# PV moved behind the MoE products of its step and one step further from its scores, with at most one MoE unit a step and a shorter distance in the last batch

## Chip, cores and metric

One NeuronCore of a Trainium2 chip runs the whole program. The metric is the device time of one execution in microseconds, median of several runs. Before the change it was 582.16 us (three runs, 581.99 to 584.43). An execution counts as slow here when it is over 1.5% above the fastest of the same kernel.

## The reference

Eight batches of attention with a threshold, then a two-layer MoE block over all tokens.

```python
scores = (1 / sqrt(64)) * q @ k.T                     # 8 batches, 8 heads, 576 x 576, head dim 64
thresh = max(scores, axis=-1) - tau                   # tau = 0.02
scores = where(scores >= thresh, scores, -1e9)
attn   = exp(scores - max) / (sum + 1e-9)
x      = (attn @ v)  as  4608 tokens x 512
h      = x @ w_in                                     # 512 -> 2048
out    = maximum(0.01 * h, h) @ w_out                 # 2048 -> 512, float32
```

## The kernel before

The engines are PE (matrix products), DVE (vector), ACT (activations), POOL (GpSimd) and SP (which issues DMAs). The program is written as one long software pipeline of 144 steps. A step computes the scores of 128 query rows for two heads; the 64 rows left over of a batch, the ragged block, go through two steps of four heads each. What happens to one step's scores, and when:

- step s: PE makes the scores (`sc`, one PSUM buffer a head). DVE scales them to `sf` with the row maximum (`mx`, then `bb`). ACT and POOL each subtract the maximum from one head's half and write the 16-bit tile `P`.
- step s+1: DVE clamps `P` as int16 (in place, `P<-P`), ACT takes the exponential into `w` with the row sums.
- step s+2: DVE takes the reciprocal of the sums (`rc`), writes it beside the weights (`w<-rc`), and the SP queue issues a DMA transpose `wt<-w`. A unit of two steps, 128 x 2560 half-precision values, is transposed at once in batches 2 to 6; batches 0 and 1, and the second half of the last, use units of one step, except for the ragged blocks.
- step s+LAG: PE multiplies the transposed weights with V (`pv`), DVE evacuates the product with the normalisation (`xT`).
- Later: the MoE. An `h` unit is 8 or 16 products into `hp`, a relu on ACT, and a leaky sum `gT` on DVE. An `o` unit is 4 products into `op`; every fourth ends in a copy `osb` and a store. Units wait in two queues and are fed one of each a step.

Each engine executes in the order in which this loop records its instructions.

```python
LAG = 5; BONUS = 0.25; NW = 4; NWT = 4; WOUT = 1; OSB_ACT = False
...
for ui in range(len(units)):
    last = units[ui][3] + size[ui] - 1
    pv_at.setdefault(EARLY.get(ui, last + LAG), []).append(ui)       # EARLY is empty
...
for s in range(NS + LAG + 1):
    credit = min(credit + 1.0 + BONUS * (len(hq) + len(oq) > 8), 2.0)
    hu, ou, fins = [], [], []
    while credit >= 1.0:            # one h and one o unit, with a backlog now and then two
        ...
    if live:
        sc = [...]                  # PE: scores
        scores(s, sc)
    ...                             # DVE: two maxima, bb; ACT and POOL: P
    leak()                          # DVE: gT of the h unit of the step before
    evacs = [pv(ui) for ui in pv_at.get(s, [])]                      # PE: PV
    for i in range(max(len(ou), len(hu))):
        if i > 0:
            leak()
        o = ou[i]() if i < len(ou) else None                         # PE: op
        h = hu[i]() if i < len(hu) else None                         # PE: hp
        if i == 0:
            for f in evacs:
                f()                                                  # DVE: xT
            evacs = []
        for f in (h, o):
            ...                                                      # ACT: relu; DVE: osb
    for f in evacs:
        f()
    ...                             # DVE: rc, w of the unit done a step ago; SP: transpose wt
    ...                             # DVE: P<-P of the step before; ACT: exp
    ...                             # loads and preparation of the next batch's q, k, v
# after the last step: the remaining o and h units, in turn
```

Of the kernel before, what the change touches and what calls it, by code (L numbers as in the profile page):

```python
# [16 lines left out]
def kernel(  # L17
# [26 lines left out]
    DM = moe_w_in.shape[0]  # L44
    DF = moe_w_in.shape[1]
    C = 1.0 / (64.0 * 64.0 * 8.0)
    LAG = 5
    NARROW = 2
    NJ = DF // 128
    NEG = -1025.0  # L50
# [1 line left out]
    NWT = 4  # L52
    NW = 4
    NP_ = 3
    BONUS = 0.25
    OSB_ACT = False
    WOUT = 1
    PT = 0
    SPOOL = 4
# [159 lines left out]
    def leak():  # L219
        for G, u, hp in leaky:  # L220
            nc.vector.scalar_tensor_tensor(  # L221
                out=G.g[u], in0=hp, scalar=0.01, in1=G.g[u], op0=AX.mult, op1=AX.add)

            nj = 512 // G.n
            nv = (u + 1) * nj // 4
            if (u + 1) * nj % 4 == 0:
                oq.append((lambda G=G, v=nv - 1: o_unit(G, v), G.n))
            if u == NJ // nj - 1:
                for v in range(NJ // 4, G.n // 32):
                    oq.append((lambda G=G, v=v: o_unit(G, v), G.n))  # L230
        leaky.clear()
# [3 lines left out]
    def osb_act():  # L235
        return OSB_ACT

# [72 lines left out]
    def group_of(b, blk):  # L310

        key = (b, blk) if blk != (4,) else ("t", b // 2)
        if key not in groups:
            groups[key] = Group([rows_of(b - b % 2 if c == 4 else b, c) for c in blk], b)
        return groups[key], (64 * (b % 2) if blk == (4,) else 0), blk != (4,) or b % 2 == 1
# [32 lines left out]
    def pv(ui):  # L348
        b, blk, p, _ = units[ui]
        wt = uwt[ui]  # L350
        vt = vts[b]
        nw = size[ui]
        if npv[0] % 2 == 0:
            pvt[0] = ps.tile([128, 2, 256], FP32, tag="pv", bufs=1, name="pv")
        pvp = pvt[0][:, npv[0] % 2, :]
        npv[0] += 1
        if p is not None:
            parts = [(p, wt[:, 0:nw, :, :], pvp[:, 0 : 128 * nw].rearrange("f (i r) -> f i r", i=nw))]
        else:
            parts = [(2 * i + u, wt[:, i : i + 1, :, ds(64 * u, 64)], pvp[:, ds(64 * (2 * i + u), 64)].rearrange("f (i r) -> f i r", i=1))  # L360
                     for i in range(2) for u in range(2)]
        for pp, w_, o_ in parts:
            for j in range(5):
                for h in range(2):
                    nc.tensor.matmul(  # L365
                        out=o_[ds(64 * h, 64)], lhsT=vt[:, pp, h, j, :], rhs=w_[:, :, 4 * h + j, :],
                        start=(j == 0), stop=(j == 4), skip_group_check=True, tile_position=(0, 64 * h))
        G, col, done = group_of(b, blk)

        def evac():  # L370


            if p is not None:
                for c in range(nw):
                    nc.vector.tensor_tensor(  # L375
                        out=G.x[:, p, ds(128 * c, 128)].rearrange("f (p i) -> f i p", i=2),
                        in0=pvp[:, ds(128 * c, 128)].rearrange("f (i p) -> f i p", i=2),
                        in1=wt[:, c, 9, :].rearrange("f (i p) -> f i p", i=2), op=AX.mult)
            else:
                x_ = G.x.rearrange("f g (p i) -> f g i p", i=2)[:, :, col // 64, :]  # L380
                nc.vector.tensor_tensor(
                    out=x_.rearrange("f (a u) p -> f a u p", u=2),
                    in0=pvp.rearrange("f (a u p) -> f a u p", a=2, u=2),
                    in1=wt[:, 0:2, 9, :].rearrange("f a (u p) -> f a u p", u=2), op=AX.mult)
            if done and (p is None or p == NP - 1):
                for u in range(NJ * G.n // 512):
                    hq.append((h_unit(G, u), G.n))

        return evac
# [11 lines left out]
    def at(s, f, t=tick):  # L401
        t.setdefault(max(0, s), []).append(f)
# [55 lines left out]
    for b in range(1, B):  # L458
        s0 = 18 * (b - 1)
        for hb in range(2):  # L460
# [7 lines left out]
            i = 0  # L468
            for nm in "kq":
                for h in range(2):  # L470
                    at(t0 + i + PT, lambda nm=nm, h=h, b=b, hb=hb: after_anchor(x64(nm, b, hb, h)), ptick)

                    def f(nm=nm, h=h, b=b, hb=hb):
                        for part in PARTS[nm]:
                            after_anchor(lo(nm, b, hb, h, part))
# [6 lines left out]

    for g in range(8):
        at(WOUT + g // 2, lambda g=g: load_w_out(g))
    EARLY = {}
    pv_at = {}
    for ui in range(len(units)):
        last = units[ui][3] + size[ui] - 1
        pv_at.setdefault(EARLY.get(ui, last + LAG), []).append(ui)

    credit = 0.0
    stores = []
# [1 line left out]
    done = None  # L494
    for s in range(NS + LAG + 1):
        live = s < NS
        for f in stores:
            f()
        stores = []

        credit = min(credit + 1.0 + BONUS * (len(hq) + len(oq) > 8), 2.0)
        hu, ou, fins = [], [], []
        while credit >= 1.0:
            f = next_o()
            if f:
                ou.append(f)
            f = next_h()
            if f:
                hu.append(f)
            credit -= 1.0  # L510

        if live:
            sc = [ps.tile([128, 1024], FP32, tag=f"sc{h}", bufs=1, name=f"sc{h}") for h in range(2)]
            scores(s, sc)
        last, prev = prev, None
        if live:
            P_ = sb.tile([128, 2, 576], FP16, tag="P", bufs=NP_, name="P")
            mx = sb.tile([128, 2], FP32, tag="mx", bufs=4, name="mx")
            sa, sB = smax(0, sc, mx), smax(1, sc, mx)
            bb = sb.tile([128, 2], FP32, tag="bb", bufs=4, name="bb")  # L520
            nc.vector.tensor_scalar(out=bb, in0=mx, scalar1=-1.0, scalar2=tau_f, op0=AX.mult, op1=AX.add)  # L521
            nc.scalar.activation(out=P_[:, 1, :], in_=sB, func=AF.Identity, bias=bb[:, 1:2], scale=1.0)  # L522
            (nc.vector if s < SPOOL else nc.gpsimd).tensor_scalar(  # L523
                out=P_[:, 0, :], in0=sa, scalar1=1.0, scalar2=bb[:, 0:1], op0=AX.mult, op1=AX.add)
            prev = (P_,) + unit_of[s]
        leak()
        evacs = [pv(ui) for ui in pv_at.get(s, [])]
        for i in range(max(len(ou), len(hu))):
            if i > 0:
                leak()  # L530
            o = ou[i]() if i < len(ou) else None
            h = hu[i]() if i < len(hu) else None
            if i == 0:
                for f in evacs:
                    f()
                evacs = []
            for f in (h, o):
                if f:
                    g_ = f()
                    if callable(g_):  # L540
                        stores.append(g_)
        for f in evacs:
            f()
        now, done = done, None
        if now is not None:
            nw = size[now]
            rc = sb.tile([128, 2, 2], FP32, tag="rc", bufs=3, name="rc")
            nc.vector.reciprocal(out=rc[:, 0:nw, :], in_=usm[now][:, 0:nw, :])  # L548
            W_ = uW[now][:, 0:nw, :]
            nc.vector.tensor_scalar(  # L550
                out=W_[:, :, 1152:1280].rearrange("p i (h r) -> p i h r", h=2),
                in0=rc[:, 0:nw, :].unsqueeze(3).to_broadcast([128, nw, 2, 64]), scalar1=1.0, scalar2=None, op0=AX.mult)
            uwt[now] = sb.tile([128, 2, 10, 128], FP16, tag="wt", bufs=NWT, name="wt")
            nc.sync.dma_start(
                out=uwt[now][:, 0:nw].rearrange("p i j r -> p (i j) r"), in_=W_.rearrange("p i c -> p (i c)"),
                transpose=True)
        if last is not None:
            P_, ui, i = last
            pi = P_.bitcast(mybir.dt.int16)
            anchor[0] = nc.vector.tensor_scalar(out=pi, in0=pi, scalar1=NEG, scalar2=None, op0=AX.max)  # L560
            if i == 0:
                uW[ui] = sb.tile([128, 2, 1280], FP16, tag="w", bufs=NW, name="w")
                usm[ui] = sb.tile([128, 2, 2], FP32, tag="sm", bufs=NW, name="sm")
            for h in range(2):
                nc.scalar.activation(  # L565
                    out=uW[ui][:, i, ds(576 * h, 576)], in_=P_[:, h, :], func=AF.Exp, bias=exp_bias, scale=1.0,
                    accum_out=usm[ui][:, i, h : h + 1])
            if i == size[ui] - 1:
                done = ui
        for t in ptick.get(s, []):  # L570
            t()
        for t in tick.get(s, []):
            t()
# [5 lines left out]
    while hq or oq or leaky:  # L579
        for nx in (next_o, next_h):  # L580
            leak()
            f = nx()
            if f:
                f = f()
# [39 lines left out]
```

## Time and profile before

The first fence is one row of the table of groups (line, engine, operation, tiles, shapes, count, then busy us and mean ns of one, then idle time before it). The second is the window view, with the run cut at the start of step 18 and of step 143; after each engine's busy time the columns are granted clock (PE's, 1.00 is full speed), DMA share and GB/s.

```profile
L560 DVE TENSOR_SCALAR P<-P 128x1152 int16<-128x1152 int16 x144 | 68.1, 473 | 0.0
```

```profile
0.00:83.60 83.60, 57.54 (x626) 37.53 (x626) 64.14 (x187) 57.85 (x117) 45.24 (x68) 0.81 1.05 195
83.60:536.90 453.30, 398.14 (x4368) 249.94 (x4369) 399.06 (x1164) 357.22 (x782) 205.85 (x269) 0.96 1.00 183
536.90:577.40 40.50, 31.99 (x336) 21.21 (x334) 17.42 (x36) 12.32 (x25) 0.75 (x1) 1.00 0.25 63
```

I call these three stretches the head, the loop (125 steps) and the tail. In the loop DVE is busy 399.06 us of 453.30 (third number with a count), so it idles 54.2 us; PE is busy 398.14. Neither engine is full.

### The profile page before, as it was taken

To read this page: it belongs to the slowest core of one execution; us is meant where nothing else is said; L and a number is where in the kernel's file an instruction comes from. 1 tells how busy PE (TensorE), PEld (TensorE's weight loads), DVE (VectorE), ACT (ScalarE), POOL (GpSimd) and SP (SyncE) were. 2 spreads that over 40 slices of the span, in tenths; PEclk is the share of its full clock that TensorE was granted. 3 is DMA by queue.
4 is the path that set the end of the run, shared out by engine and by line. 5 is a ranking of instruction groups with operands and counts; after the bars stand their busy time and mean duration, and the time that the engine had idled before them with its cause. 6 is when DMAs were issued, how large, how long until landed. Compare 5 with 4: busy or idle time off the path is not lost.

```text
span 577.4 us, 14379 instructions
## 1 busy us (share of the span) xinstructions
PE 487.7 (84%) x5328; PEld 308.7 (53%) x5328; DVE 480.6 (83%) x1385; ACT 427.4 (74%) x922; POOL 251.8 (44%) x338
## 2 busy tenths in 40 slices
PE   5549879989898779888989898976899798999896
PEld 4326546556565445555555555634566465655573
DVE  5848987999899877998879988987789799898742
ACT  5748876888789667887879877886779688787621
POOL 5335851477236741476226842376225762222100
PEclk9756988999999788998999999989899899999999
DMA  8999799999999998899997999799997999657601
GB/s 213 190 223 232 135 175 173 202 245 193 165 221 201 183 181 133 181 230 187 177 223 177 201 188 184 153 231 171 168 190 145 238 197 169 111 121 135 141 19 54
DMA packets 280133, 101.85 MB, mean 176 GB/s; under 512 B 254976, under 2 KB 267264, under 8 KB 280064
## 3 DMA queue, kind: packets, MB, share of 16 engines
q1 hardware_dynamic: 267008, 92.03, 82.9%
q0 software_dynamic: 13056, 8.92, 11.7%
q8 instruction: 41, 0.67, 0.5%
q14 instruction: 28, 0.23, 0.1%
HBM read 36.70 MB, written 9.44 MB: 80 GB/s over the span
## 4 chain that ended last, share of the span: by engine, by line
DVE 38%; DMA 27%; PE 23%; ACT 7%; issue 3%; SPq 0%; ACTq 0%
DMA wt<-w 26%; DVE sf L394 16%; PE op L239 8%; DVE gT L221 7%; PE hp L239 7%; DVE P L560 4%; ACT w L565 4%; PE sc L334 4%; DVE w L550 4%; PE pv L365 4%; DVE osb L275 3%; DVE xT L375 2%; DVE bb L521 1%; DMA qm<-in_q_dram 1%; DVE rc L548 1%
## 5 line engine op out<-in xcount | busy, mean ns | idle before, releaser
L394 DVE TENSOR_SCALAR_CACHE_REDUCE sf<-sc 128x576 f32<-128x576 f32 x288 | 205.7, 750 | 37.8 <-PE sc L334 30.0
L565 ACT ACTIVATE w<-P 128x576 f16<-128x576 f16 x288 | 193.9, 675 | 37.1 <-DVE P L560 33.5
L523 POOL TENSOR_SCALAR P<-sf,bb 128x576 f16<-128x576 f32 x140 | 106.5, 760 | 217.7 <-DVE bb L521 213.9
L239 PE MATMUL op<-wout,gT 128*128 128x512 f16 x576 | 153.4, 391 | 3.8 <-DVE osb L275 3.5
L239 PE MATMUL hp<-xT,win 128*128 128x128 f16 (+1 forms) x1600 | 155.6, 247 | 0.1
L334 PE MATMUL sc<-kst,qst 64*128 64x320 f16 (+1 forms) x1536 | 136.2, 298 | 17.1 <-DVE sf L394 13.8
L239 PEld LDWEIGHTS <-win 128*128 128x128 f16 x1600 | 125.7, 100 | 42.1 <-issue 5.6
L522 ACT ACTIVATE P<-sf,bb 128x576 f16<-128x576 f32 x144 | 111.3, 773 | 44.5 <-DVE bb L521 41.4
L253 ACT ACTIVATE gT<-hp 128x512 f16<-128x512 f32 x144 | 83.8, 583 | 55.0 <-PE hp L239 55.0
L221 DVE SCALAR_TENSOR_TENSOR gT<-hp,gT 128x512 f16<-128x512 f32 x144 | 98.5, 684 | 18.8 <-ACT gT L253 18.6
L334 PEld LDWEIGHTS <-qst 64*128 64x128 f16 x1536 | 73.7, 97 | 69.3 <-issue 44.2
L365 PE MATMUL pv<-wt,v 128*64 128x256 f16 (+2 forms) x1160 | 61.9, 246 | 57.5 <-DMA wt<-w 53.2
L365 PEld LDWEIGHTS <-v 128*64 128x64 f16 x1160 | 45.3, 114 | 77.0 <-issue 56.8
L239 PEld LDWEIGHTS <-gT 128*128 128x128 f16 x576 | 47.4, 99 | 62.9 <-issue 24.7
L560 DVE TENSOR_SCALAR P<-P 128x1152 int16<-128x1152 int16 x144 | 68.1, 473 | 0.0
L565 ACT ACTIVATION_READ_ACCUMULATOR w<-P 128x1 f32 x288 | 54.0, 188 | 0.0
L157 POOL TENSOR_TENSOR qs<-qm,qs 128x576 f16<-128x576 f32 x28 | 35.8, 1278 | 20.4 <-DVE P L560 16.3
L157 POOL TENSOR_TENSOR ks<-km,ks 128x320 f16<-128x320 f32 (+1 forms) x56 | 40.4, 742 | 9.4 <-DVE P L560 8.2
L375 DVE TENSOR_TENSOR xT<-pv,wt 128x128 f16<-128x128 f32 x128 | 33.6, 296 | 11.8 <-PE pv L365 11.5
L521 DVE TENSOR_SCALAR bb<-mx 128x2 f32<-128x2 f32 x144 | 35.2, 245 | 5.0
L550 DVE TENSOR_SCALAR w<-rc 128x256 f16<-128x256 f32 (+1 forms) x92 | 34.3, 373 | 3.2
L275 DVE COPY osb<-op 128x512 f32<-128x512 f32 x36 | 24.5, 682 | 7.5 <-PE op L239 7.5
(33 smaller groups left out, 210.2 us busy)
## 6 DMA issues: line engine op xcount, KB each, us to landing
km<-in_k_dram SPq DMA_DIRECT2D x16, 576.0 KB, 5.0
qm<-in_q_dram SPq DMA_DIRECT2D x16, 576.0 KB, 5.4
out_dram<-osb SPq DMA_DIRECT2D x36, 256.0 KB, 4.4
v<-in_v_dram POOLq DMA_DIRECT2D x16, 160.0 KB, 4.9
v<-in_v_dram POOLq DMA_DIRECT2D x16, 128.0 KB, 5.1
win<-in_moe_w_in_dram POOLq DMA_DIRECT2D x8, 256.0 KB, 8.4
wout<-in_moe_w_out_dram POOLq DMA_DIRECT2D x8, 256.0 KB, 7.9
wt<-w SPq DMA_TRANSPOSE x92, 5.3
```

The costliest lines, as they stand in the source:

```text
L157: return nc.gpsimd.tensor_tensor(out=dst[:, h], in0=src[:, h], in1=h_[:, h], op=AX.subtract)
L221: nc.vector.scalar_tensor_tensor(out=G.g[u], in0=hp, scalar=0.01, in1=G.g[u], op0=AX.mult, op1=AX.add)
L239: nc.tensor.matmul(out=out_, lhsT=lhsT, rhs=rhs, start=start, stop=stop, skip_group_check=True)
L253: nc.scalar.activation(out=G.g[u], in_=hp, func=AF.Relu, bias=0.0, scale=0.99)
L334: nc.tensor.matmul(out=sc[h][:, cols], lhsT=qt[r, g, qi, ds(2 * c, 2), :].rearrange("p t r -> p (t r)"), rhs=rhs, start=(i == 0), stop=(i ...
L365: nc.tensor.matmul(out=o_[ds(64 * h, 64)], lhsT=vt[:, pp, h, j, :], rhs=w_[:, :, 4 * h + j, :], start=(j == 0), stop=(j == 4), skip_group_ ...
L394: nc.vector.tensor_scalar(out=sf, in0=sc[h][:, ds(SC0, 576)], scalar1=C, scalar2=None, op0=AX.mult, op1=AX.max, accum_out=mx[:, h : h + 1])
L522: nc.scalar.activation(out=P_[:, 1, :], in_=sB, func=AF.Identity, bias=bb[:, 1:2], scale=1.0)
L523: (nc.vector if s < SPOOL else nc.gpsimd).tensor_scalar(out=P_[:, 0, :], in0=sa, scalar1=1.0, scalar2=bb[:, 0:1], op0=AX.mult, op1=AX.add)
L550: nc.vector.tensor_scalar(out=W_[:, :, 1152:1280].rearrange("p i (h r) -> p i h r", h=2), in0=rc[:, 0:nw, :].unsqueeze(3).to_broadcast([12 ...
L560: anchor[0] = nc.vector.tensor_scalar(out=pi, in0=pi, scalar1=NEG, scalar2=None, op0=AX.max)
L565: nc.scalar.activation(out=uW[ui][:, i, ds(576 * h, 576)], in_=P_[:, h, :], func=AF.Exp, bias=exp_bias, scale=1.0, accum_out=usm[ui][:, i, ...
```

## The change

The intent: a PV whose transpose is not there yet holds up every matmul behind it. So give the transpose more time, and put the products that need nothing from it ahead of PV.

```diff
-    LAG = 5
+    LAG = 6
-    BONUS = 0.25
+    BONUS = 0.0
+    LAGE = 4
+    ENDS = 130
...
-        pv_at.setdefault(EARLY.get(ui, last + LAG), []).append(ui)
+        lag = LAG if last < ENDS else LAGE
+        pv_at.setdefault(last + lag, []).append(ui)
...
         leak()
-        evacs = [pv(ui) for ui in pv_at.get(s, [])]
         for i in range(max(len(ou), len(hu))):
-            if i > 0:
-                leak()
             o = ...
             h = ...
-            if i == 0:
-                for f in evacs:
-                    f()
-                evacs = []
             for f in (h, o):
                 ...
-        for f in evacs:
-            f()
+        evacs = [pv(ui) for ui in pv_at.get(s, [])]
         now, done = done, None
         ...                        # rc, w, transpose; then P<-P and exp
+        for f in evacs:
+            f()
```

More of the change, by code (lines that the diff above doesn't have):

```diff
@@ L484 @@
         at(WOUT + g // 2, lambda g=g: load_w_out(g))
-    EARLY = {}
     pv_at = {}
```

## The prediction

> **What bounds the kernel now.** I read the page first (busy shares, clock row, costliest groups), then the waits, then a stretch of the timeline, then windows of 18 steps (one batch of attention). From the page:
>
> ```profile
> PE 487.7 (84%) x5328; PEld 308.7 (53%) x5328; DVE 480.6 (83%) x1385; ACT 427.4 (74%) x922; POOL 251.8 (44%) x338
> PEclk9756988999999788998999999989899899999999
> L394 DVE TENSOR_SCALAR_CACHE_REDUCE sf<-sc 128x576 f32<-128x576 f32 x288 | 205.7, 750 | 37.8 <-PE sc L334 30.0
> L365 PE MATMUL pv<-wt,v 128*64 128x256 f16 (+2 forms) x1160 | 61.9, 246 | 57.5 <-DMA wt<-w 53.2
> wt<-w SPq DMA_TRANSPOSE x92, 5.3
> ```
>
> Two engines share the bound, PE and DVE, both about 84% busy; neither is full. PE idles most ahead of PV (53.2 us, waiting for the transposed weights `wt`), DVE ahead of the row maximum (waiting for scores). `sc` has one buffer per head, so scores of step s+1 wait for the maximum of step s and the maximum waits for the scores: a late PE makes DVE late and so on round. The waits between step 18 and the last step (84 to 537 us), PE then DVE:
>
> ```profile
> PE pv L365 <- DMA wt<-w: 43.4, 28, 3.8
> PE sc L334 <- DVE sf L394: 9.6, 26, 0.8
> ...
> DVE sf L394 <- PE sc L334: 25.1, 21, 4.1
> DVE sf L394 <- PE sc L340: 7.6, 5, 3.0
> DVE gT L221 <- ACT gT L253: 6.2, 7, 1.4
> DVE xT L375 <- PE pv L365: 5.0, 5, 1.7
> ```
>
> 28 late transposes cost PE 43.4 us. DVE's listed idle there is 46.9 us with two smaller rows. One such event in the timeline:
>
> ```profile
> 213.63 1.28 PE L365 MATMUL pv<-wt,v 128*64 128x256 f16 x10 [2.61 <-DMA wt<-w]
> 214.84 1.89 PE L239 MATMUL op<-wout,gT 128*128 128x512 f16 x4
> ...
> 216.52 1.91 PE L239 MATMUL hp<-xT,win 128*128 128x256 f16 x8
> 218.37 1.45 PE L334 MATMUL sc<-kst,qst 64*128 64x320 f16 x12
> 219.86 0.76 DVE L394 TENSOR_SCALAR_CACHE_REDUCE sf<-sc 128x576 f32<-128x576 f32 x1 [4.05 <-PE sc L334]
> ```
>
> PE stood 2.61 us at PV with the MoE products behind it in the queue. Then four `op` products took 1.89 us instead of the usual 1.04 us, and DVE idled 4.05 us. The windows say why it was more than 2.61:
>
> ```profile
> 199.50:212.70 13.20, 9.90 (x112) 6.16 (x111) 10.04 (x30) 9.55 (x22) 5.80 (x7) 0.89 1.27 162
> 212.70:219.50 6.80, 5.87 (x32) 3.20 (x33) 1.97 (x7) 2.28 (x5) 0.75 (x1) 0.50 1.03 181
> 300.00:345.00 45.00, 40.48 (x433) 26.01 (x431) 40.54 (x114) 36.99 (x81) 27.87 (x37) 1.00 0.97 187
> ```
>
> After the wait the granted clock (third column from the right) was 0.50 for 6.8 us. The trace's clock record has seven such stretches after 80 us, 34 us in all.
>
> The step is the unit: 144 of them, told apart by the `bb` instruction. Step 2 starts at 23.2 us, step 18 at 83.6, the last (143) at 536.9; the end is at 577.4. Steps 18 to 143 take 3.63 us each. DVE is busy 398.8 us in 84 to 537 (sum of seven windows), 3.19 us a step. An undisturbed pair of steps, for example at 280.3 to 286.2, takes 5.9 us with DVE full.
>
> **What the Trainium skill says.** "PSUM — Partial Sum Buffer", section "Engine vs sequencer instructions": matmuls start and complete in program order, only weight loads are pulled ahead. The trace agrees: at 213.63 `op`, whose inputs do not come from this transpose, stood behind PV. "TensorE: Matmul & The Clock Gate", Part 1 (the HAM clock gate): the array runs at half clock unless it was lately busy, and an idle window of some 3.4 us puts it back. The trace shows 0.50 after a 2.61 us wait plus a shorter one before it, so agreement in kind, with a shorter single gap. "DMA: Bandwidth & Descriptors", "Rules for kernel authors", row on overlap: issue early, do compute, wait late. That is this change.
>
> **The change, part by part.** No instruction is added or removed: both built programs have 10,658 PE rows, and PV, MoE and score products are equal in number. Only order moves.
>
> (a) *PV later.* The transpose of a unit is issued two steps after the unit's last scores, some 2.5 us into the step. Before, PV stands right behind the scores three steps later (LAG 5). That leaves 3 steps less about 1.6 us, some 9 us at 3.6 us a step, minus whatever holds the queue. Its landing takes 5.3 us in the median, 7 to 9 us where loads or k and q transposes share the queue, 13.0 us once at the start. After, PV is one step later (3.2 us) and behind `op` and `hp` (1.0 and 0.9 us undisturbed): 5.1 us more. The longest of the 28 waits is 3.8 us, so all should vanish up to step 130; the 5.9 us wait at step 6, where the MoE weights are loading, should shrink to under 1 us. Without idle PE the half-clock stretches go too: 34 us at half speed lose about 17 us of PE time.
>
> (b) *The evacuation of PV (`xT`) goes to the end of DVE's step*, and PE does PV just ahead of the next scores. In double-unit batches PV at s+6 now falls in the same step as `rc` and `w`: DVE's steps become heavy (3.4 us) and light (2.5 us), where they were 3.0 and 2.9. PE's: heavy 3.35 (sc 0.9, op 0.9, hp 0.9, pv 0.7), light 2.7. The heavy ones coincide, so a pair costs about 6.1 instead of 5.9.
>
> (c) *At most one MoE unit a step.* In the order of the built programs 15 `hp` and 19 `op` units stand behind the last scores before, 17 and 23 after. Six units of about 0.9 us of PE are moved to the tail: +5.5 us there, about -2 us of DVE in the loop (two `gT` of 0.68, one `osb` of 0.68).
>
> (d) *Distance 4 at the end.* The last PV is at step 147 instead of 148; the last waits there are 2.4 us in all, and transposes of single units land in 3.4 us, so this gives about -1 us and no new wait over 1 us.
>
> **The sum.** DVE idles 453 - 399 = 54 us between steps 18 and 143. If PE were never late all of it would go. I leave some: about 6 us from light steps where PE (2.7) is above DVE (2.5), about 10 us from the 14 steps with the ragged block (two sets of score products, about 0.9 us extra of PE), and 6 to 7 us of jitter: 23 us. So 54 + 2 - 23 = 33 us saved. Steps 2 to 17 take 60.4 us against about 50 of DVE work; I take 8 us. The tail costs 5.5 - 1 = 4.5 us more. Span: 577.4 - 33 - 8 + 4.5 = 540.9. The measured time is 582.2 - 577.4 = 4.8 us over the span, so 545.7; I say 545 us, 6.4% less. That is 3.37 us a step in 18 to 143.
>
> **The rivals.**
> 1. *The transpose only lands later.* The DMA share is about 1.0 in most slices, and a faster loop asks the same 101.85 MB in less time. If the rings were full, the wait would come back and the gain would be 1 to 2% (570 to 576 us). For it: landings of 7 to 9 us in busy stretches. Against it: in 300 to 310 us the share falls to 0.51, and waits of the issuing queue for DVE's `w` add up to 111.2 us, so it starves more than it is full.
> 2. *DVE takes over at once.* The 43 us of PE waiting may be mostly hidden behind a busy DVE, since listed DVE idle is only 46.9 us, and a delayed evacuation is one more place where DVE, in order, stands ahead of the next maximum. At 3.5 us a step: 125 x 3.5 = 437 against 453, so about 561 us. For it: steps at 3.5 to 3.9 us with no listed wait (an `osb`, a long `bb` beside POOL). Against it: DVE's busy sum is 3.19 a step.
> 3. *The tail eats the gain.* More MoE units left at the end, where DVE waits for ACT 12.2 us in the trace. At 3 us a pair for three pairs, +9 us rather than +5.5: 549 us. A slower result than before would need this and rival 1 together.
> 4. *Everything overlaps.* DVE full at 3.2 us a step: another 20 us less, 525 us.
>
> **Range and chances.** Between rival 4 in part and rival 2: 529 to 563 us. Under 570.5 us (2% faster) needs only a quarter of the 54 us, so 0.93; within 2%, 0.06; slower, 0.01.
>
> **What would show it.** Right: the row PV waiting for `wt` under 8 us in all, no half-clock stretch after 90 us, DVE over 90% busy from step 18 on at 3.3 to 3.45 us a step, the part behind the last `bb` about 45 us (was 40.5). Step (a) is wrong if PV still waits for `wt` over 15 us; (b) if DVE waits for PV ahead of `xT` by more than 10 us; (c) if the part behind the last `bb` is over 50 us.

## The result

The changed kernel takes 547.49 us in the median (four runs, 545.67 to 548.97), beside 582.08 us for the kernel before in the same rounds. The ratio is 0.9417, 95% interval 0.9345 to 0.9489. A ratio here is the mean time of one kernel's fast runs over that of the other's fast runs of the same rounds, so it is not quite the ratio of the medians quoted. The prediction was 545 us.

The page of the changed kernel, the rows that answer to those in the prediction, and the clamp:

```profile
PE 484.4 (89%) x5328; PEld 305.0 (56%) x5328; DVE 491.3 (90%) x1385; ACT 423.4 (77%) x922; POOL 253.2 (46%) x338
...
PEclk9655998999999989999999999999999999999999
...
L396 DVE TENSOR_SCALAR_CACHE_REDUCE sf<-sc 128x576 f32<-128x576 f32 x288 | 204.7, 746 | 11.0 <-PE sc L336 10.9
...
L367 PE MATMUL pv<-wt,v 128*64 128x256 f16 (+2 forms) x1160 | 59.1, 240 | 8.0 <-DMA wt<-w 7.3
...
L554 DVE TENSOR_SCALAR P<-P 128x1152 int16<-128x1152 int16 x144 | 82.9, 576 | 0.0
...
wt<-w SPq DMA_TRANSPOSE x92, 5.6
```

PV waits 7.3 us for transposes instead of 53.2, the row maximum idles 11.0 us instead of 37.8, and the clock row is full from the sixteenth slice on. The transposes themselves got no faster: 5.6 us to landing against 5.3. One row went the wrong way: the clamp `P<-P` takes 576 ns instead of 473, with the same instruction and the same count.

The waits of the loop (80 to 507 us), PE then DVE:

```profile
PE sc L336 <- DVE sf L396: 18.9, 50, 1.2
...
PE pv L367 <- DMA wt<-w: 1.8, 3, 1.3
...
DVE sf L396 <- PE sc L336: 5.3, 5, 2.4
```

The roles are exchanged. Before, DVE waited for scores that PE could not make; now PE waits 50 times, some 0.4 us each, for DVE to let go of the score buffer. DVE is now busy for 97% of the loop; e8 and e11 below test whether it is the only bound. The same three stretches as before:

```profile
0.00:83.20 83.20, 59.37 (x626) 37.36 (x626) 64.32 (x185) 57.31 (x116) 45.86 (x68) 0.77 1.09 198
83.20:503.70 420.50, 388.60 (x4348) 244.08 (x4348) 408.02 (x1163) 352.65 (x780) 206.60 (x269) 0.99 1.07 196
503.70:546.50 42.80, 36.40 (x362) 23.60 (x358) 18.97 (x38) 13.46 (x26) 0.74 (x1) 1.00 0.26 67
```

| stretch | before | after | difference | predicted |
|---|---|---|---|---|
| head (steps 0 to 17) | 83.6 | 83.2 | -0.4 | -8 |
| loop (steps 18 to 143) | 453.3 | 420.5 | -32.8 | -33 |
| of it, DVE idle | 54.2 | 12.5 | -41.7 | -31 |
| of it, DVE busy | 399.1 | 408.0 | +8.9 | -2 |
| tail | 40.5 | 42.8 | +2.3 | +4.5 |
| span of the profiled run | 577.4 | 546.5 | -30.9 | -36.5 |

So in these two profiles the whole gain is in the loop, where DVE idles 42 us less and works 9 us more. (The loop is steadier than the head: e4, whose program is the same as far as step 130, has a loop of 420.5 us too, but a head of 80.2.)

**Where DVE's extra work comes from.** First a step before the change, then one after. The lines give the start, the duration, the engine and the instruction.

```profile
280.41 0.68 DVE L221 SCALAR_TENSOR_TENSOR gT<-hp,gT 128x512 f16<-128x512 f32 x1
...
280.67 0.74 POOL L523 TENSOR_SCALAR P<-sf,bb 128x576 f16<-128x576 f32 x1 [2.23 <-DVE bb L521]
281.01 0.49 DVE L375 TENSOR_TENSOR xT<-pv,wt 128x128 f16<-128x128 f32 x2
...
281.41 0.45 DVE L560 TENSOR_SCALAR P<-P 128x1152 int16<-128x1152 int16 x1
```

```profile
233.34 0.68 DVE L223 SCALAR_TENSOR_TENSOR gT<-hp,gT 128x512 f16<-128x512 f32 x1
...
233.61 0.74 POOL L525 TENSOR_SCALAR P<-sf,bb 128x576 f16<-128x576 f32 x1 [1.36 <-DVE bb L523]
233.95 0.72 DVE L554 TENSOR_SCALAR P<-P 128x1152 int16<-128x1152 int16 x1
```

Before, either `xT` or `rc` and `w` stood between `gT` and the clamp, alternately, and POOL's instruction on the next `P` tile was over when the clamp began. In the new order `xT` comes behind the clamp, so a step without `rc` and `w` has neither ahead of it, and the clamp starts at 233.95 while POOL works until 234.35. (LAG 6 alone has the same effect: the evacuation of a two-step unit then falls in the same step as `rc` and `w`; see e1 and e2.) In the whole trace 66 clamps overlap a POOL instruction by more than 150 ns and take 727 ns in the mean, the other 78 take 448 ns. Before it was 19 (638 ns) and 125 (448 ns). That the two compete for something is what the Trainium skill says ("SBUF — State Buffer", section "Who interferes with whom": a two-port mode of DVE on SBUF operands and a GpSimd instruction share a port pair, and whoever issues first holds the other up for its whole instruction). The trace agrees in kind: POOL, which was first, keeps its 0.74 us, and DVE is the longer one. So it is in 58 of the 66 (clamp 765 ns in the mean). In the other 8 the two began within 0.1 us of each other; there the clamp kept its 450 ns and POOL's instruction took 1.02 to 1.08 us, as here:

```profile
251.73 0.44 DVE L554 TENSOR_SCALAR P<-P 128x1152 int16<-128x1152 int16 x1
251.76 1.02 POOL L525 TENSOR_SCALAR P<-sf,bb 128x576 f16<-128x576 f32 x1
```

That the clamp runs in such a mode is not shown by a run. In the loop the clamp alone costs 14.4 us more than before; shorter `bb` and maxima give some of it back.

**Why the head gained little or nothing.** At step 7, in order of time:

```profile
42.16 0.74 PE L367 MATMUL pv<-wt,v 128*64 128x128 f16 x10 [5.13 <-DMA wt<-w]
42.20 0.68 ACT L559 ACTIVATE w<-P 128x576 f16<-128x576 f16 x1 [5.74 <-DMA wt<-w]
...
43.67 0.17 DVE L542 RECIPROCAL rc<-sm 128x2 f32<-128x2 f32 x1 [5.16 <-ACT w L559]
```

The second transpose landed 14.3 us after its issue. PV waits as before, only a step later, and the same landing now also holds ACT: the exponential of a later unit needs the `w` buffer that this transpose reads (there are four), and DVE stands behind ACT at `rc` for 5.16 us. More distance for PV doesn't help a wait that comes through another buffer. The stand varies between profiles: in e4, whose program is the same here, `rc` waits 4.1 us. So between these kernels a difference of the head under some 3 us says nothing.

### The profile page after: what moved, and what is told of

Read it like the earlier page. It is cut to its first block, busy times and chain, and to the rows that moved or that the text cites. A ratio compares the mean times of both kernels' runs of the same rounds, so it can differ in the third digit from the quotient of the medians.

```text
span 546.5 us, 14352 instructions
## 1 busy us (share of the span) xinstructions
PE 484.4 (89%) x5328; PEld 305.0 (56%) x5328; DVE 491.3 (90%) x1385; ACT 423.4 (77%) x922; POOL 253.2 (46%) x338
## 5 line engine op out<-in xcount | busy, mean ns | idle before, releaser
L396 DVE TENSOR_SCALAR_CACHE_REDUCE sf<-sc 128x576 f32<-128x576 f32 x288 | 204.7, 746 | 11.0 <-PE sc L336 10.9
L525 POOL TENSOR_SCALAR P<-sf,bb 128x576 f16<-128x576 f32 x140 | 107.8, 770 | 196.9 <-DVE bb L523 179.6
L336 PE MATMUL sc<-kst,qst 64*128 64x320 f16 (+1 forms) x1536 | 142.2, 298 | 30.5 <-DVE sf L396 23.7
L241 PE MATMUL hp<-xT,win 128*128 128x128 f16 (+1 forms) x1600 | 153.8, 244 | 2.9 <-DVE xT L377 2.7
L241 PE MATMUL op<-wout,gT 128*128 128x512 f16 x576 | 149.1, 382 | 7.8 <-DVE osb L277 4.6
L241 PEld LDWEIGHTS <-win 128*128 128x128 f16 x1600 | 124.0, 99 | 45.1 <-issue 7.9
L336 PEld LDWEIGHTS <-qst 64*128 64x128 f16 x1536 | 77.6, 97 | 81.0 <-issue 54.3
L554 DVE TENSOR_SCALAR P<-P 128x1152 int16<-128x1152 int16 x144 | 82.9, 576 | 0.0
L367 PE MATMUL pv<-wt,v 128*64 128x256 f16 (+2 forms) x1160 | 59.1, 240 | 8.0 <-DMA wt<-w 7.3
L367 PEld LDWEIGHTS <-v 128*64 128x64 f16 x1160 | 40.4, 112 | 25.4 <-issue 14.5
L544 DVE TENSOR_SCALAR w<-rc 128x256 f16<-128x256 f32 (+1 forms) x92 | 36.5, 396 | 3.2
L277 DVE COPY osb<-op 128x512 f32<-128x512 f32 x36 | 24.5, 680 | 4.1 <-PE op L241 4.1
```

Of the source, the lines that this page charges most:

```text
L241: nc.tensor.matmul(out=out_, lhsT=lhsT, rhs=rhs, start=start, stop=stop, skip_group_check=True)
L336: nc.tensor.matmul(out=sc[h][:, cols], lhsT=qt[r, g, qi, ds(2 * c, 2), :].rearrange("p t r -> p (t r)"), rhs=rhs, start=(i == 0), stop=(i ...
L367: nc.tensor.matmul(out=o_[ds(64 * h, 64)], lhsT=vt[:, pp, h, j, :], rhs=w_[:, :, 4 * h + j, :], start=(j == 0), stop=(j == 4), skip_group_ ...
L396: nc.vector.tensor_scalar(out=sf, in0=sc[h][:, ds(SC0, 576)], scalar1=C, scalar2=None, op0=AX.mult, op1=AX.max, accum_out=mx[:, h : h + 1])
L525: (nc.vector if s < SPOOL else nc.gpsimd).tensor_scalar(out=P_[:, 0, :], in0=sa, scalar1=1.0, scalar2=bb[:, 0:1], op0=AX.mult, op1=AX.add)
L554: anchor[0] = nc.vector.tensor_scalar(out=pi, in0=pi, scalar1=NEG, scalar2=None, op0=AX.max)
```

## The experiments

Twelve kernels ran, each on one chip together with the kernel before. All gave a correct result. One run of the kernel before (586.6 us) was slow and is left out of the ratios. The question: which of the parts carries the gain, and is what is left the bound that the profile names? "Loop" is the time from step 18 to 143 in the profiled run. The head varies from 79.2 to 88.0 us among these profiles, so single spans are compared less than loops.

| run | median us | ratio to before | loop us | PV's waits for `wt` in the loop | clamp ns |
|---|---|---|---|---|---|
| before | 582.1 | | 453.3 | 43.4 | 473 |
| changed | 547.5 | 0.942 | 420.5 | 1.8 | 576 |
| e1 distance alone | 560.5 | 0.967 | 434.2 | 8.7 | 558 |
| e2 order alone | 565.3 | 0.975 | 439.3 | 21.2 | 537 |
| e10 no bonus alone | 574.5 | 0.993 | 444.1 | 50.5 | 477 |
| e9 distance, no bonus | 551.0 | 0.951 | 426.0 | 14.0 | 563 |
| e3 changed with bonus | 557.2 | 0.962 | 434.5 | 3.0 | 556 |
| e7 changed with LAG 5 | 561.9 | 0.966 | 438.3 | 32.0 | 520 |
| e4 changed, long end | 546.2 | 0.944 | 420.5 | 0.5 | 572 |

**e1, the distance alone.** On the kernel before:

```diff
-    LAG = 5
+    LAG = 6
```

> The kernel before with LAG 6 alone (PV still right behind the scores, bonus units kept, distance 6 to the end). Theory 'distance': 27 of the 28 waits for wt after step 18 are shorter than one step (3.3 us), so PV's waits for wt fall from 53 us to under 15 us, half-clock stretches after 90 us nearly vanish, and the time is 552 to 562 us; it stays some 5 to 10 us over the changed kernel. Rival 'order': what counts is that no matmul stands behind PV; then DVE still idles over 35 us ahead of the row maximum and the time is 568 to 582.

Measured: 560.5 us, ratio 0.9672 (0.9622 to 0.9722). One row of the groups:

```profile
L365 PE MATMUL pv<-wt,v 128*64 128x256 f16 (+2 forms) x1160 | 60.5, 243 | 18.6 <-DMA wt<-w 13.6 <-DVE rc L548 3.4 <-DVE xT L375 0.5
```

The waits fall from 53.2 to 13.6 us and the time into the range of the theory "distance". One number alone brings 19.1 of the loop's 32.8 us. It stays further behind the changed kernel (13 us) than expected, and 17 us of half clock are left in the loop, where nearly none were expected. The clamp is already long here (558 ns), with PV and the evacuation in their old places. In e2, where only the place within the step changes, it is long too (537 ns): either change alone takes away what stood ahead of the clamp.

**e2, the order alone.** On the kernel before, PV behind the products and `xT` at the end of the step:

```diff
-        evacs = [pv(ui) for ui in pv_at.get(s, [])]
         for i in range(max(len(ou), len(hu))):
...
-            if i == 0:
-                for f in evacs:
-                    f()
-                evacs = []
...
-        for f in evacs:
-            f()
+        evacs = [pv(ui) for ui in pv_at.get(s, [])]
...
+        for f in evacs:
+            f()
```

> The kernel before with PV behind the MoE products and its evacuation at the end of the step, LAG 5 and bonus units kept. Theory 'distance': the order gives only 2 us more, which covers the shorter half of the 28 waits; PV's waits for wt 12 to 25 us, 556 to 568 us. Rival 'order': PV behind the products takes the whole gain, 546 to 553 us.

Measured: 565.3 us, ratio 0.9746 (0.97 to 0.9792); PV's waits are 21.2 us in the loop. The row of the waits of the whole run (us in total, times, longest):

```profile
PE pv L365 <- DMA wt<-w: 29.3, 17, 5.9
```

The time and the waits in the loop are in the range of the theory "distance" (29.3 us in the whole run is a little over it): the order acts as some 2 us more of slack.

**e3, the bonus units back.** On the changed kernel:

```diff
-    BONUS = 0.0
+    BONUS = 0.25
...
         for i in range(max(len(ou), len(hu))):
+            if i > 0:
+                leak()
```

> The changed kernel with the bonus units (0.25) back. By the order of the programs 14 hp and 19 op units (208 and 76 products) stand behind the last scores instead of 17 and 23. Theory: a unit costs DVE 0.68 us wherever it stands and the loop is DVE-bound, so the loop gets 2 to 5 us longer and the tail some 4 us shorter: 544 to 550 us, same within 1%. Rival 'bonus units stall the loop' (a step with two units cost 5 to 6 us before): 552 to 558 us.

Measured: 557.2 us, ratio 0.962 (0.9571 to 0.9669), beside 0.9442 for e4 on the same chip. My theory fell, and the rival's range holds. The tail is 37.3 us against 42.8, the 5.5 us that I had worked out; but the loop is 14.0 us longer, though DVE is busy only 2.2 us more in it. Eight loop steps carry two units; by the times between `bb` instructions they take 4.4 to 6.4 us, 5.19 in the mean, against 3.36 for the average step of the changed kernel: 8 x 1.83 = 14.6 us. One of them, in the timeline:

```profile
288.23 0.68 DVE L223 SCALAR_TENSOR_TENSOR gT<-hp,gT 128x512 f16<-128x512 f32 x1
...
288.96 1.05 PE L241 MATMUL hp<-xT,win 128*128 128x256 f16 x8 [0.18 <-DVE gT L223]
289.12 0.57 ACT L255 ACTIVATE gT<-hp 128x512 f16<-128x512 f32 x1
289.72 0.69 DVE L223 SCALAR_TENSOR_TENSOR gT<-hp,gT 128x512 f16<-128x512 f32 x1 [0.82 <-ACT gT L255]
...
290.33 0.68 DVE L277 COPY osb<-op 128x512 f32<-128x512 f32 x1
```

The second `gT` must stand behind ACT's relu of the same step (0.82 us of idle DVE), and the scores of the next step stand behind twice the products. Nor does the extra unit stay gained: 122 relus fall in the loop against 119, since the queue is empty sooner and later steps have none.

**e4, the long distance to the end.** On the changed kernel:

```diff
-    LAGE = 4
+    LAGE = 6
```

> The changed kernel with distance 6 to the end instead of 4. The last PV moves from step 147 to 149 and with it the MoE units of the last group. Theory: the tail has enough older units to fill the two steps, so +0 to 3 us (547 to 551). Rival 'the short end is worth two whole steps': +6 us or more (553 and over).

Measured: 546.2 us, ratio 0.9442 (0.9391 to 0.9494), just under the range expected. The loop is the same, 420.5 us, and the tail 43.3 us against 42.8. The short end is worth nothing that shows. As its loop is that of the changed kernel, this run stands for it beside e1 to e3, which ran on the same chip.

**e7, LAG 5 in the changed kernel.**

```diff
-    LAG = 6
+    LAG = 5
```

> The changed kernel with LAG 5 in place of 6 (order, no bonus, short end kept). Theory: slack falls by one step to 9 us, landings of 7 to 9.7 us then reach PV again: PV's waits for wt 8 to 20 us, time +2 to +8 us (549 to 556). Rival 'the order alone covers the landings': waits under 8 us and, as rc/w and xT then fall in different steps, the same time or better (543 to 548).

Measured: 561.9 us, ratio 0.9664 (0.9619 to 0.9709), PV's waits 39.6 us in all. Worse than either theory had it. The order and the missing bonus without the distance keep 15.0 of the loop's 32.8 us. In time they are worth as much as the distance alone (0.9664 and 0.9672): each covers part of what the other covers.

**e9 and e10, the missing corners.** On the kernel before: e9 sets LAG 6 and BONUS 0, e10 only BONUS 0.

```diff
-    LAG = 5              # e9 alone
+    LAG = 6
-    BONUS = 0.25         # e9 and e10
+    BONUS = 0.0
```

> The kernel before with LAG 6 and no bonus units, PV still right behind the scores. It separates the order from the other two parts. In the single-part runs, distance with bonus gave 3.47 us a step, and adding the order to it 3.48. Theory 'distance and no bonus carry it, the order adds little': 3.36 to 3.40 us a step, 546 to 553 us, some 8 us of waits for wt left. Rival 'the order is what lets the missing bonus pay': 3.44 us a step or more, 555 us and over.

> The kernel before with the bonus units taken away and nothing else. A bonus step took 5.2 us against 3.4 in the run that had them back (8 such steps, 14.6 us); the tail pays 4 to 5 us for them. Theory 'the two-unit steps stall by themselves': 571 to 576 us. Rival 'at distance 5 the two-unit steps give the transposes time, so their absence returns as waits for wt': waits for wt over 48 us and 577 to 584 us.

Measured: e9 551.0 us, ratio 0.9511 (0.9452 to 0.957), 3.41 us a step, PV's waits 14.0 us in the loop. The time is in the theory's range, the step a little above it, and the waits are above the 8 us expected. e10 574.5 us, ratio 0.9927 (0.9871 to 0.9983). PV's row of the waits in e10, whole run:

```profile
PE pv L365 <- DMA wt<-w: 59.3, 39, 5.6
```

In e10 the time is the theory's (571 to 576) and the waits are the rival's (50.5 us in the loop, over 48): the two-unit steps do stall, but without them the transposes have less time, and PV's waits in the loop grow by 7.1 us. Put together, the parts don't add. By differences of ratios: bonus removed alone 0.7%, with the distance 1.6% (0.9672 to 0.9511), with distance and order 2.0% (0.962 to 0.942). The order gives 2.5% alone, 0.5% with the distance (e1 to e3), and 0.9% on top of distance and no bonus (e9 to the changed kernel), the last two with overlapping intervals, so not shown.

**e5, the second MoE weights loaded later.** On the changed kernel:

```diff
-    WOUT = 1
+    WOUT = 6
```

> The changed kernel with the loads of the second MoE weights begun at step 6 instead of 1. Theory: the 5.2 us stand at step 7 (rc waits for ACT's exp, which waits for the w buffer of a transpose that landed 14.3 us after issue) comes from these loads sharing the DMA rings with the first transposes; the landing falls under 9 us, the stand under 1 us, time -4 to -6 us (542 to 544). Rival 'the first transposes are slow in themselves or because of the first MoE weights': landing stays over 11 us, time within 1.5 us of the changed kernel.

Measured: 553.1 us, ratio 0.9501 (0.9441 to 0.9562). From its waits, whole run:

```profile
DVE rc L542 <- ACT w L559: 10.8, 6, 4.6
```

Half right: the mechanism held, and the time missed its range by 9 us. The stand at step 7 is gone, so the loads were its cause; but they now meet later transposes of the narrow units, and DVE and PE stand at steps 10, 11 and 12 instead. DVE waits for ACT at `rc` 10.8 us instead of 6.0, and the slowest landing is 18.5 us instead of 14.3.

**e6 and e12, the clamp out of POOL's way.** On the changed kernel, LAG 7 and `xT` ahead of the clamp, so that each step has something between `gT` and the clamp; e12 has a fifth `wt` buffer as well.

```diff
-    LAG = 6
+    LAG = 7
-    NWT = 4             # e12 alone
+    NWT = 5
...
+        for f in evacs:
+            f()
         if last is not None:       # P<-P, exp
...
-        for f in evacs:
-            f()
```

> The changed kernel with LAG 7 and the evacuation xT ahead of the int16 maximum P<-P, so that rc and w stand ahead of P in one step and xT in the other. Theory 'P collides with POOL': P<-P (576 ns mean, 0.45 or 0.72) goes back to 450 to 490 ns, DVE is busy 10 to 14 us less; DVE is the bound, so the loop gains up to 12 us unless xT now waits for PV: 538 to 546 us. Rival 'P's length is chance': mean stays over 550 ns.

> The run with LAG 7 and xT ahead of P, with a fifth wt buffer. P fell from 576 to 493 ns there and DVE was busy 6 us less, but the waits of scores for qst (10.0 us) and of rc for ACT (4.1 us, plus 3.9 at step 7) took it back. Theory 'the issuing queue stood at transposes without a free wt buffer, and all behind it came late': qst waits under 5 us, rc waits under 1 us, P still under 500 ns, 540 to 547 us. Rival 'seven steps are too many for other reasons': qst and rc waits stay, 551 us and over.

Measured: e6 558.05 us with one slow run among the four, ratio of the fast runs 0.9538 (0.9448 to 0.9628). e12 549.1 us, ratio 0.948 (0.9427 to 0.9532). So e6 misses its range by 12 us, and e12 lies between the ranges of theory and rival. First the clamp in e6, then in e12, then two waits of e12:

```profile
L556 DVE TENSOR_SCALAR P<-P 128x1152 int16<-128x1152 int16 x144 | 71.0, 493 | 0.0
```

```profile
L556 DVE TENSOR_SCALAR P<-P 128x1152 int16<-128x1152 int16 x144 | 72.5, 503 | 0.0
```

```profile
PE sc L336 <- DMA qst<-qs: 10.6, 7, 3.0
...
DVE xT L377 <- PE pv L367: 5.7, 7, 1.6
```

The clamp is short again, 493 and 503 ns, and DVE is busy 402.7 us in e12's loop against 408.0: this part of the theory stands. But the time was not gained. With four buffers scores waited 10.0 us for the transposed queries and `rc` 9.8 us for ACT; the fifth buffer took `rc`'s waits out of the loop (4.1 us of the 9.8) and 7.1 us off the loop (429.0 to 421.9), yet the waits for `qst` stayed at 10.6 us. So my reason for those, an issuing queue held by transposes without a free buffer, is not their cause. What makes them late is open.

**e8 and e11, the output copy on ACT.** On the changed kernel; e11 also puts the copy ahead of the relu on ACT and loads one piece of the second MoE weights a step.

```diff
-    OSB_ACT = False
+    OSB_ACT = True
...
-            for f in (h, o):                      # e11 alone
+            for f in (o, h):
...
-        at(WOUT + g // 2, lambda g=g: load_w_out(g))   # e11 alone
+        at(WOUT + g, lambda g=g: load_w_out(g))
```

> The changed kernel with the output copy osb on ACT instead of DVE (36 copies, 24.5 us of DVE). Theory 'DVE is now the bound': DVE loses about 24 us of work, ACT gains 36 x 0.6 = 21 us (to about 81% busy), the loop gains until PE (3.1 to 3.2 us a step) binds: -8 to -16 us, 532 to 540 us. Rival 'coupled, no single bound': within 1% (542 to 553).

> The changed kernel with osb on ACT and issued there ahead of the relu of the same step, and the second MoE weights loaded one piece a step instead of two. With osb on ACT behind the relu, PE waited 18.6 us for the copy ahead of op, and the loop gained only 2.7 us. Theory: with the copy first, this wait falls under 6 us and the loop goes to 3.24 to 3.30 us a step; the slower loads spare the first transposes up to 5 us: 530 to 539 us. Rival 'DVE relieved, the next bound is close behind': 540 to 546.

Measured: e8 543.3 us, ratio 0.9348 (0.9284 to 0.9412); e11 540.2 us, ratio 0.9356 (0.9301 to 0.9411). Both lie in the ranges of the rivals. Waits of e8, then of e11:

```profile
PE op L241 <- ACT osb L275: 22.7, 29, 1.4
```

```profile
PE pv L367 <- DMA wt<-w: 17.7, 15, 3.4
...
PE op L241 <- ACT osb L275: 10.2, 15, 1.1
```

The copies took DVE 24.5 us. In e8 it is busy 20.5 us less in the whole run and 14.8 us less in the loop, and little of that arrives: the loop is 417.8 us in e8 and 417.6 in e11, against 420.5. So DVE was not the only bound. In e8 PE waits for ACT's copy to free the one `op` bank. With the copy first this halves, and waits for transposes take its place. The expectation for e11 failed by a microsecond in the median and clearly in the loop (3.34 us a step, not 3.24 to 3.30). Both are the fastest kernels, but their intervals overlap with that of the changed kernel (0.9345 to 0.9489), so that they beat it is likely and not shown. They were run at other times. They beat the kernel before by 6.5%.

## Why the prediction was right, and where it erred

The time (545 against 547.5), the direction and the mechanism of the main part were right; the nearness of the number is in part luck. Of the signs that it named, PV's waits (7.3 us, under 8), DVE's share of the loop (97%) and the step (3.36 us) held; one half-clock stretch after 90 us was left (3.4 us, at 194.8), and the tail was 42.8 us for about 45. By its own steps:

- **(a) PV later: right in kind, and the main part.** It said that all waits vanish up to step 130: 43.4 us became 1.8 in the loop. The half-clock stretches between step 18 and 143 fell from 34 to 7 us. (They begin inside the waits, not after them as the prediction reads its example: see the last section.) e1 and e9 show that the distance does most of this (8.7 and 14.0 us of waits left), and e7 that without it most of the waits stay (32.0). In time the distance is not alone: e7 gains as much without it as e1 does with it alone.
- **The head: wrong.** "Should shrink to under 1 us" was said of the wait at step 6, and 8 us were put into the sum. The wait is still 5.1 us, a step later, and of the 8 came 0.4 us in these two profiles, 3.4 beside e4's head. The reading took PV's own slack for the only path; the same late landing reaches DVE through the `w` buffer.
- **(b) The heavy and light steps: right, its size missed.** The changed trace mostly has steps of 2.8 and 3.3 to 4.4 us in turn, as said; a pair takes 6.7 us in the mean, ragged steps included, where 6.1 was put down for a plain one. That DVE's busy time would stay the same was wrong: 399 became 408 us, because the clamp meets POOL in most light steps. I had taken the durations of the light step from a trace in which the two met in 19 of 144 steps.
- **(c) The bonus units: the tail right, the loop mis-sized.** "+5.5 us there" is what e3 shows (37.3 against 42.8). "About -2 us of DVE in the loop" was the term that failed: it is 14.0 us, as a two-unit step stalls by 1.8 us. I counted a unit's work and not the chain of products, relu and leaky sum that has to fit within one step.
- **(d) The short end: right to expect little.** e4 finds about 0.5 us.
- **The sum.** Idle left in the loop was put at 23 us and is 12.5; extra DVE work was put at -2 us and is +8.9. These two errors, of 10.5 and 10.9 us, cancel, so the loop came out at -32.8 for a predicted -33 with half of its reasoning off. The missing 7.6 us of the head were partly offset by the tail (2.2 us better than put down; e2, with the order alone, has a tail shorter by the same amount). The 4.8 us "over the span" were a misreading: they are the median of three runs less the span of another run, which itself took 579.39 us, 2.0 over its span. From profiled run to profiled run the span fell by 30.9 us, not by 36.5; the medians hide most of that miss.
- **The rivals.** Number 1 (the rings are full) is refuted: landings rose only from 5.3 to 5.6 us while DMA moved 186 GB/s instead of 176. Number 2 (DVE takes over at 3.5 us a step) and number 3 (a tail 9 us longer) did not come: 3.36 us a step, and 2.3 us. Number 4 (all overlaps) came nearest for DVE's idle time, which was its point, and failed by DVE's longer work.

## What to carry to other kernels

A wait on an in-order engine is paid by everything queued behind it, so lengthen the distance first and reorder second: here one more step of distance alone gave 3.3% and the new order alone 2.5%, with intervals that just touch. When the last slack goes, look again at each instruction's mean duration, since moving one instruction can make another one longer by bringing it beside an engine that it shares a port with. And ask of a late transfer which buffers it holds: a consumer moved away from it is no help to the producer that waits for the buffer.

## What the Trainium skill lacked or had wrong

- "SBUF — State Buffer", "Who interferes with whom": the rule holds here, but its figures are of single instructions in tests, and there is none for what it costs a schedule. With POOL first, 58 times in the changed kernel, the clamp took 765 ns instead of 448; 8 times, with the two begun together, POOL's instruction took over 1.02 us instead of 0.75. The clamp's share of the loop rose by 14.4 us.
- "TensorE: Matmul & The Clock Gate", Part 1: an idle window of some 3.4 us is named as what brings the half clock. Here the clock fell to 0.50 for 6.8 us at 212.70, 1.7 us into a single gap of 2.61 us (211.02 to 213.63), after 3.41 us in which PE had been busy for 1.41. The loop before the change had 34 us of such time with no listed wait of PE over 3.8 us. In the loops of all 14 traces 47 falls are on record; before each, PE was busy for 3 to 49% of the last 3.41 us, and no such stretch of full clock, cut on the record's own grid of 3.41 us, with over 51% was followed by one. So a window that is a little more than half idle was enough here.
- "DMA: Bandwidth & Descriptors": its fit of time against bytes is for another issuing path and for plain copies, and for transposes it has a bandwidth but no time to landing, alone or beside other transfers. For transposes from SBUF to SBUF, 92 of them, the runs show 3.3 us at the least from issue to landing, 5.6 in the median and 14.3 beside the loads of the weights in the changed kernel. The issuing instruction alone takes 1.25 to 6.4 us of the queue (3.1 in the median).
